# The first block's keys move from SyncE's queue to GpSimd's, in an attention-and-MLP kernel whose order is a searched list

## The chip, the cores and the metric

The program runs on one core of one Trainium2 chip. The metric is the device time in microseconds (us) of one execution. Three executions of the kernel before took 229.1, 229.35 and 229.35 us.

The engines are called PE (TensorE), DVE (VectorE), ACT (ScalarE), POOL (GpSimd) and SP (SyncE). Each runs its own instructions strictly in the order in which they were written, and a wait holds up everything that is queued behind it on that engine. DMAs are issued from two queues here: POOL's, where each issue is itself an instruction that takes 0.5 to 0.9 us of POOL, and SP's.

## The reference

```
scores = (q @ k.T) / sqrt(64)                # 4 batches, 8 heads, 768 positions, 64 wide
keep   = key is one of the first 4, or is among the 128 up to and including the query
a      = softmax(where(keep, scores, -1e9))
x      = (a @ v), heads side by side         # 3072 x 512
h      = x @ w_in                            # 512 x 2048
g      = h * sigmoid(1.702 * h)
out    = g @ w_out                           # 2048 x 512
```

Inputs and output are fp32; the kernel computes its matrix products in fp16.

## The kernel before

**Tiles.** There are 24 blocks of 128 positions, six to a batch. A window of 128 means that a block needs its own keys, those of the block before it in its batch, and the four "sink" keys of the batch. The kernel takes the blocks in the order `ORDER` = 0, 6, 12, 18, 1, 2, 3, ...: the four first blocks of the batches, which have no block before them, come first. This text counts blocks by their **place** in that order, 0 to 23, and writes q3, k3, v3 for the loads of place 3. Two places make a group for the MLP, 12 groups in all. The loads of w_in and w_out come in four quarters each: i0 to i3 and o0 to o3.

**One place, from end to end.** POOL loads q, k and v; such a load turns fp32 into fp16 on its way. Queries and keys are transposed: by PE with a copy by DVE or ACT (places 0 to 7, "tq", L398 and L405, copies at L355 and L359) or by a DMA of SP (L433). PE makes the scores (L481, "own" and, from place 4 on, "prv" for the block before, and L510 for the sinks). DVE merges the two halves (L527), takes maxima (L537, L554, L557) and subtracts them (L578, L602). ACT takes the exponential (L617). The result is transposed by PE (places 0 to 5, L657) or by a DMA of SP ("at", L682); POOL zeroes what the window leaves out (L620, L624). PE multiplies with v (L715, L719, and L709 for the sinks, "av"), DVE divides by the sum (L726, L727, "xn"), and a second transpose follows, by PE (L745) or, for two places at once, by a DMA of SP ("xT", L758).

**The MLP of a group.** PE multiplies with w_in (L780, "hT", steps of 16 or 8 matmuls), ACT applies the gate (L810; for places 0 and 1 ACT takes a tanh at L794 and DVE finishes at L801), PE multiplies with w_out (L834, "o", steps of four matmuls), DVE or ACT copies the sum out (L355, L359) and SP sends it to DRAM.

**Buffers.** The scores' PSUM tile "own" exists once: the next place's scores may start only when DVE has subtracted the maxima of the place before. "mm", for hT, o and transposes, exists three times. POOL's DMAs in flight are limited: the trace shows POOL waiting, before a new issue, for an earlier load to land.

**What sets the order.** Nothing is scheduled when the program is built. A list `SEQUENCE` of 834 operations names, for each, its number and its engine (p PE, a ACT, d DVE, t POOL, s SP), and the kernel emits them in just that order. The list was found by a search off the chip that used the costs in the calls of `plan.add` (cost on the engine, `xfer` for a transfer, `post` for the delay until its data may be used). The costs themselves emit no instruction.

**The first block's keys.** In the kernel before, `hw=["k0"]` sends k0 another way than all other loads: SP loads it as fp32 into a tile of its own, `raw_k` (L263), and DVE rounds it to fp16 (L271, in `round16`). q0 and the other loads of places 0 to 3 are issued by POOL at L277 (128 rows of 512 values), later ones of q and k at L284, of v at L255, w_in at L293, w_out at L302.

Of the kernel before, what the change touches and what calls it, by code (L numbers as in the profile page):

```python
# [27 lines left out]
PE, ACT, DVE, POOL, SP = "PE", "ACT", "DVE", "POOL", "SP"  # L28
# [8 lines left out]
    gbatch={},  # L37
    tanh=(0, 1),
    last=(256, 128, 128),
    hw=["k0"],  # L40
    big=(0, 1, 2, 3),
    avb={0: ("mi", "mm"), 1: ("mi", "mm"), 2: ("mi", "mm")},
    hb={},
# [4 lines left out]
    slack={'v': 1, 's': 1, 'x': 1, 'e': 0.0, 'p': 0.0},  # L48
    steady=8,
    after=8.0,  # L50
    loads="q0 q1 k1 q2 k2 q3 k3 v0 v1 i0 i1 v2 v3 i2 i3 o0 o1 q4 k4 v4 o2 q5 k5 v5 o3".split(),
)
RING = dict(qkn=4, qkt=4, qk0=2, e32=4, a16=4, at=4, atp=4, xn=2, xt=4, gt=3, osb=4, mm=3, own=1, pv=1, mi=1, th=2)

SEQUENCE = """
0s 10d 4d 37s 12t 7d 14t 11a 16t 13t 106p 38d 15t 9d 2d 103p 6d 23t 3d 101p 104a 20t 126p 102a 18t 107p 127d 17t
124p 19t 108d 149p 109d 125a 22t 147p 150a 110d 129p 25t 148a 130p 111d 112a 105t 131d 113a 114p 132d 170p 115a 26t
116p 133d 171a 118p 152p 21t 117a 119d 153p 135a 134d 29t 120p 8d 137p 136a 121d 172p 33t 138a 154d 122p 173a 30t  # L60
139p 156d 123a 175p 155d 174t 140a 141p 481p 142d 158a 24t 157d 143p 176p 482a 144d 160p 34t 159a 483d 145p 161a 27t
177d 162p 484p 163a 146d 28t 179d 166p 487p 485a 167d 181a 486d 493p 488a 178d 489d 490p 40t 494a 180d 39t 478p 491a
495d 182a 32t 492d 183p 164p 479a 165d 499p 36t 184a 480d 185p 42t 500a 187p 195p 186d 193p 501d 48t 189p 196a 496p
190d 194a 168p 188d 497a 217p 215p 197p 169a 498d 218a 198p 191p 43t 199d 514p 192a 508p 216d 515a 200d 518p 46t
201d 509p 519a 31t 202d 239p 502p 240a 52t 203d 219p 128t 237p 221d 503p 238a 204a 520p 67t 222d 220p 510p 5d 223d
93s 504p 225d 224d 1s 242p 49t 94s 511p 151d 226a 45t 505p 512d 241p 521a 51t 506d 516p 243d 54t 524p 517a 244d 205p
525a 528p 206d 253p 245d 529a 255p 207t 522p 254d 247d 256a 246d 530p 35t 523a 227p 97t 208p 248a 228d 258p 257p
209d 270s 531p 259d 210t 230p 532p 260d 231a 229t 211p 261d 526p 249s 232t 212d 533p 527a 263d 262d 44t 233p 60t
536p 234d 264a 55t 213p 534d 537p 214d 41t 271p 538p 50t 273d 265s 235p 250t 539p 236a 274d 272p 548p 540a 296s 275d
550p 276d 57t 549a 552p 58t 277d 283p 53t 553a 544p 285d 551a 266t 554p 545a 286d 284p 251p 555a 287d 542p 61t 252d  # L70
546p 47t 288d 267p 56t 547a 556p 543a 268d 564p 289d 557a 269s 278a 558p 541s 297p 559p 299d 290a 565p 279s 300d
298p 566p 535s 301d 560p 96s 302d 291s 567p 303d 309p 304a 280t 95s 561p 311d 568a 305s 310p 578p 562d 570p 312d
579a 322s 292t 576p 98d 281p 571a 572p 66t 282d 584p 306t 313d 573a 507s 577a 513s 293p 585a 580p 294d 64t 574p 314d
581a 295s 84t 592p 575a 315d 316a 63t 307p 593p 59t 308d 586p 73t 317s 582p 72t 594p 99t 583a 587p 70t 323p 604p
325d 348s 595p 605a 326d 588p 596a 318t 324p 600p 327d 328d 589p 601a 598p 329d 65t 590d 335p 591s 78t 608p 563s
337d 62t 612p 609a 338d 69t 599a 336p 602p 613a 68t 339d 319p 603a 341d 340d 82t 606p 76t 620p 320d 607a 85t 342a
614p 100d 321s 79t 610p 361p 75t 330a 621p 343s 363d 91t 615p 611a 364d 331s 362p 616p 365d 622p 367d 366d 617p 623p
618a 632p 374s 624d 638p 636p 344t 639a 349p 637a 630p 351d 350p 626p 631a 352d 332t 345p 627a 634p 633a 346d 628p
353d 81t 640p 354d 629a 635a 333p 368a 648p 334d 642p 355d 347s 375p 356a 643p 569s 377d 641a 376p 357s 649p 378d
644p 369s 379d 650p 380d 645p 625s 656p 619s 646d 597s 381d 387p 358t 657a 400s 662p 389d 668p 663a 370t 651p 669a  # L80
359p 652a 388p 654p 360d 77t 658p 390d 74t 660p 659a 391d 80t 655a 371p 393d 392d 661a 71t 664p 372d 676p 665a 382a
373s 401p 670p 403d 647s 402p 671p 404d 394a 383s 666p 405d 677p 667a 406d 395s 672p 407d 413p 408a 673p 415d 384t
684p 674d 678p 416d 685a 409s 414p 679p 90t 417d 426s 692p 87t 680d 385p 418d 693a 396t 696p 419d 386d 686p 682p 88t
687a 397p 410t 683a 690p 697a 398d 688p 691a 399s 698p 689a 420a 694p 411p 699p 412d 695a 421s 700p 427p 675s 710p
429d 452s 712p 711a 430d 428p 701p 713a 422t 431d 720p 432d 724p 721a 702d 439p 725a 86t 433d 718p 441d 92t 716p
719a 442d 83t 440p 714p 717a 89t 423p 715a 732p 434a 424d 704p 443d 425s 445d 733p 444d 435s 722p 446a 705p 723a
681s 465p 447s 706p 467d 734p 703s 468d 466p 750p 436t 469d 735p 751a 470d 707p 736a 448t 742p 708a 746p 743a 437p
747a 738p 438d 748p 471d 739a 449p 749a 740p 472a 450d 744p 451s 453p 726p 745a 473s 455d 727p 456d 737s 454p 728p
741a 653s 457d 760p 459d 458d 752p 474t 729p 753a 460a 761p 730d 772p 762p 773a 461s 766p 763p 767a 780p 764a 770p
475p 462t 771a 768p 781a 476d 776p 769a 778p 777a 788p 779a 463p 774p 464d 782p 775a 477s 789p 765s 783p 731s 784p  # L90
790p 785p 796p 786d 791p 797a 754p 792a 808p 793s 709s 794p 787s 809a 802p 795a 755p 803a 806p 756p 807a 798p 800p
799a 757p 801a 804p 758d 822p 759s 805a 810p 816p 811p 823p 812p 824p 813p 817p 814a 825p 818p 826a 815s 828p 819p
827s 829p 820d 830p 831p 821s 832a 833a
"""


# [69 lines left out]
def kernel(  # L166
# [28 lines left out]
    plan = Plan(RING)  # L195
# [26 lines left out]
    def by(e):  # L222
        return nc.sync if e == SP else nc.scalar
# [19 lines left out]
    )  # L243

    def sw(key, cost, fn, xfer, **kw):
        return plan.add(POOL, key, cost, fn, xfer=xfer, post=0.9, **kw)

    ld, qkn = {}, {}

    def load_block(which, b, key, after=0.0):  # L250
        bb, r = divmod(b, 6)
        pair, i = divmod(PLACE[b], 2)
        src = {"q": q, "k": k, "v": v}[which][bb, :, r * P : (r + 1) * P, :].rearrange("h s d -> s h d")
        if which == "v":
            return sw(key, 0.88, lambda b=b, x=2: nc.gpsimd.dma_start(v65[:, b, :, 0:D], src), 0.88 if pair < 4 else 0.95, deps=[z_1], after=after)  # L255
        w = "qk".index(which)
        buf = qkn[pair]
        if which + str(PLACE[b]) in CFG["hw"]:
            raw = const.tile([P, H * D], FP32, name=f"raw_{which}{b}")
            n = CFG["hw"].index(which + str(PLACE[b]))  # L260
            src = {"q": q, "k": k}[which][bb, :, r * P : (r + 1) * P, :].rearrange("h (t e) d -> t h (e d)", e=8)
            got = plan.add(
                {SP: 0.45, ACT: 0.6}, -120 + n, 0, lambda e, src=src, raw=raw, x=9: by(e).dma_start(raw, src), xfer=0.75, post=0.6  # L263
            )

            def round16(e, b=b, w=w, i=i):
                dst, src = buf()[:, i, w].rearrange("p h d -> p (h d)"), raw
                if e == ACT:
                    nc.scalar.copy(out=dst, in_=src)
                else:  # L270
                    (nc.vector if e == DVE else nc.gpsimd).tensor_copy(out=dst, in_=src)  # L271

            return plan.add({DVE: 0.42, ACT: 0.6, POOL: 0.8}, -110 + n, 0, round16, deps=[got], take=[buf])
        if PLACE[b] in CFG["big"]:
            return sw(
                key, 0.64,
                lambda b=b, w=w, i=i: nc.gpsimd.dma_start(  # L277
                    buf()[:, i, w].rearrange("p h d -> p (h d)"),
                    {"q": q, "k": k}["qk"[w]][bb, :, r * P : (r + 1) * P, :].rearrange("h (t e) d -> t h (e d)", e=8),
                ),  # L280
                0.7, take=[buf], after=after,
            )
        return sw(
            key, 0.88, lambda b=b, w=w, i=i: nc.gpsimd.dma_start(buf()[:, i, w], src), 0.88 if pair < 4 else 0.95,  # L284
            take=[buf], after=after,
        )
# [4 lines left out]
    def load_w_in(f, key):  # L291
        def go(f=f, x=0):
            nc.gpsimd.dma_start(  # L293
                w_in16[:, :, bass.ts(f, 512)],
                moe_w_in.rearrange("(c p) f -> p c f", p=P)[:, :, bass.ts(f, 512)],
            )

        return sw(key, 0.8, go, 2.5)

    def load_w_out(f, key):  # L300
        def go(f=f, x=1):
            nc.gpsimd.dma_start(  # L302
                w_out16[:, bass.ts(f, 4)],
                moe_w_out[bass.ts(f, 512), :].rearrange("(c p) f -> p c f", p=P),
            )

        return sw(key, 0.8, go, 2.5)

    for n, what in enumerate(CFG["loads"]):
        w, x = what[0], int(what[1:])  # L310
# [2 lines left out]
        key = -100 + n  # L313
# [581 lines left out]
```

## Time and profile before

| | us |
|---|---|
| three timed executions, median | 229.35 (229.1 to 229.35) |
| the profiled execution, its own time | 228.31 |
| its span in the profile | 226.6 |
| PE busy | 214.5 (95%) |
| DVE busy, ACT busy, POOL busy | 136.2, 136.6, 113.5 |
| granted TensorE clock | 1.0 |
| DMA queue 0 (POOL's loads) | 79.6% of 16 engines |
| DMA queue 1 (SP's) | 44.7% of 16 engines |

The times of single instructions below come from the one profiled execution, whose own time is 1.04 us under the median; differences are worked out inside the profile and then added to the median. "Busy" time of PE counts matmuls that overlap, so that the mean duration of a group (257 ns for one matmul of hT) is more than it costs when matmuls follow each other: eight hT matmuls in a row take 0.87 us and four of o 0.86 us in the chain of waits.

### The profile page before, as it was taken

To read this page: it belongs to the slowest core of one execution; us is meant where nothing else is said; L and a number is where in the kernel's file an instruction comes from. 1 tells how busy PE (TensorE), PEld (TensorE's weight loads), DVE (VectorE), ACT (ScalarE), POOL (GpSimd) and SP (SyncE) were. 2 spreads that over 40 slices of the span, in tenths; PEclk is the share of its full clock that TensorE was granted. 3 is DMA by queue.
4 is the path that set the end of the run, shared out by engine and by line. 5 is a ranking of instruction groups with operands and counts; after the bars stand their busy time and mean duration, and the time that the engine had idled before them with its cause. 6 is when DMAs were issued, how large, how long until landed. Compare 5 with 4: busy or idle time off the path is not lost.

```text
span 226.6 us, 5625 instructions
## 1 busy us (share of the span) xinstructions
PE 214.5 (95%) x2378; PEld 151.7 (67%) x2378; DVE 136.2 (60%) x243; ACT 136.6 (60%) x190; POOL 113.5 (50%) x135
## 2 busy tenths in 40 slices
PE   1889899999999999999899999999999999999994
PEld 0658876776784785675675685686765956856763
DVE  0899898998896852796286677843957371111010
ACT  2588696796746766367349249848585669613511
POOL 8955654698980689397071670780816112300000
PEclk9999999999999999999999999999999999999999
DMA  6999999999999999999998998999998072042112
GB/s 128 174 205 196 178 191 191 156 142 137 134 164 157 203 210 156 120 219 134 148 174 133 260 138 144 127 147 130 150 116 198 4 191 38 17 138 77 66 46 93
DMA packets 123512, 32.47 MB, mean 143 GB/s; under 512 B 114880, under 2 KB 120416, under 8 KB 123488
## 3 DMA queue, kind: packets, MB, share of 16 engines
q0 software_dynamic: 71792, 13.51, 79.6%
q1 hardware_dynamic: 51552, 18.55, 44.7%
q8 instruction: 18, 0.29, 0.6%
q10 hardware_dynamic: 144, 0.07, 0.1%
q14 instruction: 6, 0.05, 0.1%
HBM read 27.46 MB, written 6.29 MB: 149 GB/s over the span
## 4 chain that ended last, share of the span: by engine, by line
PE 77%; DMA 10%; POOL 5%; DVE 2%; ACT 1%; SPq 1%; issue 1%; POOLq 0%; DVEq 0%
PE o L834 33%; PE hT L780 31%; DMA w_in<-in_moe_w_in_dram 6%; DMA at<-a 4%; PE own L481 3%; PE av L715 2%; PE av L719 2%; PE av L709 2%; PE prv L481 2%; POOL qkn L277 2%; SPq L682 1%; POOL v L255 1%; POOL w_in L293 1%; PE tq L405 1%; PE snk L510 1%
## 5 line engine op out<-in xcount | busy, mean ns | idle before, releaser
L780 PE MATMUL hT<-xT,w_in 128*128 128x256 f16 (+1 forms) x896 | 94.1, 257 | 1.4 <-DMA xT<-xn 0.6
L834 PE MATMUL o<-w_out,gT 128*128 128x512 f16 (+2 forms) x416 | 91.8, 363 | 0.0
L810 ACT ACTIVATE gT<-hT 128x512 f16<-128x512 f32 x88 | 50.9, 597 | 58.7 <-PE hT L780 58.4
L780 PEld LDWEIGHTS <-w_in 128*128 128x128 f16 x896 | 75.3, 98 | 14.5 <-DMA xT<-xn 1.1
L834 PEld LDWEIGHTS <-gT 128*128 128x128 f16 x416 | 37.2, 98 | 32.2
L620 POOL TENSOR_SCALAR_AFFINE_SELECT atp<-at 128x1024 f16<-128x1024 f16 (+1 forms) x22 | 22.2, 1009 | 65.7 <-DMA at<-a 64.7
L527 DVE COPY_PREDICATED own<-consts,prv 128x1024 f32<-128x1024 uint16 x20 | 24.6, 1229 | 24.3 <-PE prv L481 24.2
L537 DVE TENSOR_REDUCE mx<-own 128x8 f32<-128x1024 f32 (+1 forms) x28 | 29.7, 1068 | 0.9 <-PE own L481 0.4
L578 DVE TENSOR_TENSOR e<-own,mx 128x1024 f32<-128x1024 f32 (+1 forms) x28 | 29.8, 1066 | 0.9
L617 ACT ACTIVATE a<-e 128x1056 f16<-128x1056 f32 (+1 forms) x28 | 26.2, 952 | 4.9 <-issue 2.6
L624 POOL TENSOR_SCALAR_AFFINE_SELECT at<-at 128x1024 f16<-128x1024 f16 (+1 forms) x22 | 22.5, 1024 | 1.5
L355 DVE COPY osb<-o 128x512 f32<-128x512 f32 (+1 forms) x12 | 8.0, 666 | 24.3 <-PE o L834 24.3
L284 POOL DMA_DIRECT2D qkn<-in_k_dram x20 | 17.8, 902 | 7.4 <-DMA w_out<-in_moe_w_out_dram 5.1
L255 POOL DMA_DIRECT2D v<-in_v_dram x24 | 21.4, 902 | 0.0
L726 DVE RECIPROCAL rcp<-av 128x8 f32<-128x8 f32 (+1 forms) x28 | 5.5, 195 | 26.5 <-PE av L719 26.4
L284 POOL DMA_DIRECT2D qkn<-in_q_dram x20 | 17.8, 894 | 2.3 <-DMA qkn<-in_k_dram 0.7
L810 ACT ACT_TABLE_LOAD x14 | 18.0, 1283 | 0.2
L727 DVE TENSOR_TENSOR xn<-av,rcp 128x512 f16<-128x512 f32 (+1 forms) x28 | 17.2, 615 | 1.0
L715 PE MATMUL av<-v,at 128*128 128x65 f16 x192 | 17.0, 194 | 0.6 <-POOL at L624 0.5
L617 ACT ACT_TABLE_LOAD x13 | 16.7, 1283 | 0.2
L715 PEld LDWEIGHTS <-at 128*128 128x128 f16 x192 | 14.2, 98 | 2.5 <-POOL at L624 1.2
L481 PEld LDWEIGHTS <-qkT 64*128 64x128 f16 x352 | 10.2, 96 | 7.8 <-issue 5.1
(56 smaller groups left out, 165.9 us busy)
## 6 DMA issues: line engine op xcount, KB each, us to landing
out_dram<-osb SPq DMA_DIRECT2D x23, 256.0 KB, 2.5
qkn<-in_q_dram POOLq DMA_DIRECT2D x24, 128.0 KB, 5.3
v<-in_v_dram POOLq DMA_DIRECT2D x24, 128.0 KB, 5.6
qkn<-in_k_dram POOLq DMA_DIRECT2D x23, 128.0 KB, 8.6
w_in<-in_moe_w_in_dram POOLq DMA_DIRECT2D x4, 512.0 KB, 10.2
w_out<-in_moe_w_out_dram POOLq DMA_DIRECT2D x4, 512.0 KB, 11.6
at<-a SPq DMA_TRANSPOSE x18, 3.3
raw_k<-in_k_dram SPq DMA_DIRECT2D x1, 256.0 KB, 4.6
```

What stands on the lines that cost most here:

```text
L255: return sw(key, 0.88, lambda b=b, x=2: nc.gpsimd.dma_start(v65[:, b, :, 0:D], src), 0.88 if pair < 4 else 0.95, deps=[z_1], after=after)
L284: key, 0.88, lambda b=b, w=w, i=i: nc.gpsimd.dma_start(buf()[:, i, w], src), 0.88 if pair < 4 else 0.95,
L527: nc.vector.copy_predicated(out=own(lo, hi).rearrange("p l j s -> p (l j) s"), mask=later.unsqueeze(1).to_broadcast((P, 4 * (hi - lo), P)) ...
L537: lambda lo=lo, hi=hi, own=half, small=small: nc.vector.tensor_reduce(out=small[:, lo:hi], in_=own(lo, hi), axis=AX.X, op=ALU.max),
L578: nc.vector.tensor_tensor(out=e32()[:, 512 * lo : 512 * hi].rearrange("p (l j s) -> p l j s", j=4, s=P), in0=own(lo, hi), in1=small[:, lo: ...
L617: nc.scalar.activation(out=a16()[:, lo:hi], in_=e32()[:, lo:hi], func=AF.Exp, scale=scale)
L620: nc.gpsimd.affine_select(out=atp()[:, lo : lo + n], in_=at()[:, lo : lo + n], pattern=[[0, n], [-1, P]], compare_op=ALU.is_gt, fill=0.0, ...
L624: nc.gpsimd.affine_select(out=at()[:, lo : lo + n], in_=at()[:, lo : lo + n], pattern=[[0, n], [1, P]], compare_op=ALU.is_ge, fill=0.0, ba ...
L715: nc.tensor.matmul(acc[:, j], at()[:, c], v65[:, b, h], start=(r == 0), stop=(r == 0))
L780: nc.tensor.matmul(ht()[:, n], w_in16[:, c, bass.ts(f, P)], xt[g]()[:, tok, c], start=(c == 0), stop=(c == 3))
L810: lambda fs=fs, cols=cols, gt=gt, ht=ht: nc.scalar.activation(out=gt()[:, fs[0] : fs[-1] + 1, cols], in_=ht(), func=AF.Gelu_apprx_sigmoid),
L834: nc.tensor.matmul(po(), gt()[:, F, bass.ts(t, P)], w_out16[:, F, cols], start=(F == 0), stop=(F == NF - 1))
```

## The change

k0 is loaded by POOL like the other keys, at L277, as POOL's first DMA, and lands as fp16. SP's load L263 and DVE's cast L271 are gone (their code stays, unused). Some costs that only the search reads were changed, and the list was searched again: it has 833 operations on the same engines, with another order on each of them.

```diff
-    hw=["k0"],
+    hw=[],
...
-    loads="q0 q1 k1 q2 k2 q3 k3 v0 v1 i0 i1 ...".split(),
+    loads="q0 k0 q1 k1 q2 k2 q3 k3 v0 v1 i0 i1 ...".split(),
...
-        return plan.add(POOL, key, cost, fn, xfer=xfer, post=0.9, **kw)
+        return plan.add(POOL, key, cost, fn, xfer=xfer, **{"post": 1.1, **kw})
...
-                {SP: 0.45, ACT: 0.6}, ... by(e).dma_start(raw, src), xfer=0.75, post=0.6
+                {SP: 0.45, ACT: 0.6}, ... by(e).dma_start(raw, src), xfer=0.9, post=0.6
...
-                key, 0.64,                     # q and k of places 0 to 3
+                key, 0.56,
...
-        return sw(key, 0.8, go, 2.5)           # w_in, w_out
+        return sw(key, 0.8, go, 2.5, post=2.0)
```

The two lists, decoded for the queues that the prediction speaks of. "sink3" is the copy of the sink keys of place 3 (L448), "sel" POOL's zeroing (L620, L624), "tr12" SP's transpose of the queries and keys of places 12 and 13 (L433), "at" L682, "xT" L758.

```
POOL, from the start
  before: q0 k1 k2 q1 q2 v2 v1 k3 q3 v0 i1 i2 sink0 i3 i0 q4 q5 k4 sink3 v3 k5 o0 o1 k6 q6 o2 o3
  after:  k0 q0 k2 q1 q2 k1 k3 q3 v1 v0 i1 i2 i3 v2 sink2 i0 k4 v3 q4 sink1 q5 k5 o0 k6 q6 o1 o2 o3
SP, from the start
  before: consts raw_k ...          after: own-mask consts ...
DVE, from the start
  before: 3 memsets, round k0, 4 memsets, copy k1, maxima and subtractions of place 0 ...
  after:  6 memsets, copy q0, copy k2, maxima and subtractions of place 0 ...
PE, from the start
  before: mask0, tq k0, tq q0, tq k1, own0, tq q1, tq k2, tq q2, mask1, own1 ...
  after:  mask0, tq k0, tq q0, tq k2, own0, tq q1, tq k1, tq k3, mask1, own1 ...
SP, places 8 to 10
  before: at8, at9, at10, tr12 (an output and loads of sink values between)
  after:  at8, at9, tr12, at10, one output ahead of at8
POOL and SP, places 11 to 14
  before: sel11, then 11 loads; SP xT10/11, at13, at12, tr16; POOL sel13, sel12, q20; SP xT12/13
  after:  sel11, then 5 loads; SP at12, xT10/11, at13, tr16; POOL sel12, sel13, then 8 loads; SP xT12/13
POOL and SP, places 16 to 18
  before: SP at16, at17, at18, tr20; POOL sel16, 2 loads, sel17, sel18
  after:  SP at16, at17, tr20, at18; POOL sel16, sel17, sel18
```

More of the change, by code (lines that the diff above doesn't have):

```diff
@@ L50 @@
     after=8.0,
-    loads="q0 q1 k1 q2 k2 q3 k3 v0 v1 i0 i1 v2 v3 i2 i3 o0 o1 q4 k4 v4 o2 q5 k5 v5 o3".split(),
+    loads="q0 k0 q1 k1 q2 k2 q3 k3 v0 v1 i0 i1 v2 v3 i2 i3 o0 o1 q4 k4 v4 o2 q5 k5 v5 o3".split(),
 )
@@ L57 @@
 SEQUENCE = """
[L58 to L92, printed above, removed]
@@ L93 @@
-827s 829p 820d 830p 831p 821s 832a 833a
+1s 6d 0s 4d 13t 3d 12t 17t 14t 2d 8d 10d 16t 11a 15t 105p 19t 18t 102p 21t 100p 103a 20t 148p 101d 23t 106p 149d 26t
+123p 107d 125p 27t 124a 9d 108d 171p 126a 24t 109d 128p 110d 129p 111a 7d 172a 130d 113p 169p 112a 131d 146p 114a
+133d 147a 115p 117p 132d 116a 151p 150t 118d 134a 119p 152p 120d 22t 170a 154d 135a 121p 31t 136p 122a 174p 156d
+175p 25t 137a 153d 138p 480p 177d 139a 30t 155d 158a 142p 483p 127t 481a 143d 157a 482d 140p 34t 484a 159p 141d 161p
@@ new lines @@
+160a 35t 485d 162a 163p 176d 144p 28t 486p 145a 178d 39t 165p 179d 492p 487a 166d 180a 488d 493a 182p 181a 5d 494d
+489p 38t 92s 183d 29t 184p 490a 477p 185d 33t 491d 188p 192p 478a 164d 194p 37t 186p 498p 193a 479d 104t 195a 187d
+495p 499a 189d 42t 167p 500d 496a 196p 41t 168a 216p 497d 214p 190p 217a 198d 513p 191a 60t 197p 215d 507p 514a 199d
+173t 517p 200d 48t 518a 501p 201d 51t 236p 238p 202d 218p 239a 44t 508p 237a 220d 203a 219p 519p 221d 502p 32t 222d
+509p 223d 503p 224d 240p 225a 45t 510p 520a 47t 504p 511d 36t 242d 241p 523p 505a 53t 527p 243d 524a 50t 204p 528a
@@ new lines @@
+521p 244d 40t 205a 246d 245d 515p 522a 96t 254p 516a 252p 206t 529p 255d 247a 253d 207p 226p 269s 208d 256p 209t
+530p 258d 227a 525p 259d 228t 229p 526a 210p 248s 230d 257p 531p 211d 231t 535p 260d 262d 54t 261d 232p 46t 536p
+233d 263a 52t 532p 43t 234p 533d 270p 537p 249t 272d 235a 264s 212p 271p 538p 213a 273d 547p 62t 539a 274d 549p 540s
+275d 548a 295s 551p 276d 282p 265t 550a 555p 284d 543p 556a 94s 285d 552a 283p 57t 250p 93s 544a 286d 541p 59t 251d
+545p 49t 542a 287d 266p 56t 546a 553p 267d 74t 557p 288d 554a 268s 277a 296p 558p 298d 512s 297p 559p 299d 289a 278s
@@ new lines @@
+563p 98t 300d 560p 301d 290s 564p 561d 321s 565p 302d 303a 308p 279t 577p 310d 569p 304s 578a 97d 566p 291t 311d
+534s 280p 567a 579p 281d 77t 573p 580a 78t 292p 574a 309p 570a 583p 58t 312d 293d 575p 305t 584a 313d 294s 571p 581p
+572a 55t 306p 582a 63t 591p 576a 307d 66t 585p 314d 315a 61t 322p 603p 65t 324d 592p 325d 604a 316s 593p 323p 594p
+506s 326d 328d 607p 327d 595a 586p 347s 608a 599p 334p 600a 601p 317t 336d 568s 611p 602a 337d 335p 605p 612a 69t
+338d 597p 606a 340d 72t 339d 318p 598a 81t 587p 329a 319d 68t 609p 71t 360p 588p 341a 330s 362d 619p 610a 589d 320s
@@ new lines @@
+361p 620p 363d 613p 364d 621p 365d 342s 614p 622p 331t 562s 615p 95s 623d 348p 624s 616p 373s 350d 343t 625p 366d
+351d 349p 635p 626a 617a 631p 352d 85t 636a 637p 632a 75t 344p 70t 627p 345d 83t 633p 354d 628a 64t 332p 634a 67t
+639p 638a 333d 80t 629p 353d 346s 76t 647p 630a 640a 374p 355a 641p 376d 648p 377d 642p 367a 356s 375p 649p 378d
+379d 650p 590s 368s 667p 380d 651a 386p 668a 596s 643p 388d 399s 357t 661p 389d 644p 662a 655p 645a 369t 387p 663p
+656a 390d 358p 664a 659p 73t 359d 653p 84t 391d 370p 79t 654a 392d 657p 660a 371d 665p 99d 658a 372s 381a 400p 669p
@@ new lines @@
+646s 402d 675p 403d 393a 401p 382s 670p 404d 666a 676p 405d 394s 671p 406d 425s 412p 407a 677p 414d 383t 413p 683p
+415d 672p 684a 416d 678p 408s 395t 418d 384p 673a 681p 385d 695p 679d 396p 680s 696a 685p 682a 397d 409t 687p 417d
+686a 398s 691p 89t 689p 692a 688a 86t 410p 690a 697p 90t 419a 411d 715p 82t 693p 87t 716a 698p 420s 426p 674s 699p
+428d 694a 652s 719p 429d 427p 711p 720a 451s 430d 709p 712a 431d 421t 717p 710a 432d 438p 718a 713p 440d 439p 703p
+714a 441d 723p 442d 422p 724a 444d 700p 433a 423d 721p 443d 424s 704p 701d 445a 434s 464p 731p 722a 466d 446s 465p
@@ new lines @@
+705p 467d 732p 468d 706p 470d 435t 469d 733p 707a 747p 708s 749p 91t 734p 447t 750a 748a 436p 735a 739p 437d 88t
+745p 448p 746a 741p 740a 449d 743p 450s 737p 744a 742a 618s 452p 738a 725p 454d 751p 455d 759p 752a 471a 453p 726p
+456d 457d 775p 760p 458d 459a 472s 727p 776a 761p 460s 728p 762p 729d 771p 473t 763a 767p 769p 768a 461t 474p 770a
+777p 772a 475d 765p 778a 773p 766a 462p 774a 787p 463d 781p 476s 779p 730s 788p 780a 702s 782p 764s 789p 783p 790p
+797p 791a 784p 792s 798a 736s 803p 785d 805p 786s 804a 795p 806a 807p 796a 793p 808a 801p 794a 799p 802a 821p 800a
@@ L94 @@
+753p 822p 809p 754p 823p 755p 824p 810p 825a 826s 815p 811p 816p 812p 756p 813d 817p 814s 757a 827p 818p 758s 828p
+819d 829p 830p 820s 831a 832a
 """
@@ L262, in load_block @@
             got = plan.add(
-                {SP: 0.45, ACT: 0.6}, -120 + n, 0, lambda e, src=src, raw=raw, x=9: by(e).dma_start(raw, src), xfer=0.75, post=0.6
+                {SP: 0.45, ACT: 0.6}, -120 + n, 0, lambda e, src=src, raw=raw, x=9: by(e).dma_start(raw, src), xfer=0.9, post=0.6
             )
@@ L305, in go @@
             )
-        return sw(key, 0.8, go, 2.5)
+        return sw(key, 0.8, go, 2.5, post=2.0)
     for n, what in enumerate(CFG["loads"]):
```

## The prediction

> **What bounds the kernel now.** The page first: the span, the engines' shares and the slices.
>
> ```profile
> span 226.6 us, 5625 instructions
> ...
> PE 214.5 (95%) x2378; PEld 151.7 (67%) x2378; DVE 136.2 (60%) x243; ACT 136.6 (60%) x190; POOL 113.5 (50%) x135
> ...
> PE   1889899999999999999899999999999999999994
> ...
> DMA  6999999999999999999998998999998072042112
> ```
>
> PE is the bound: away from the first slices and the last it hardly rests, at a granted clock of 1.0. DMA is full in nearly every slice up to about 170 us. The change takes no matmul away, so the time can move only by PE's idle stretches. The waits of PE show which there are:
>
> ```profile
> PE own L473 <- DMA consts<-cconst: 2.9, 1, 2.9
> PE tq L398 <- DVE qkn L271: 2.4, 1, 2.4
> PE hT L780 <- DMA xT<-xn: 0.6, 1, 0.6
> PE hT L780 <- DMA w_in<-in_moe_w_in_dram: 0.6, 1, 0.6
> ...
> PE av L715 <- POOL at L624: 0.5, 1, 0.5
> ```
>
> The second is what the change is about. Fourth: PE at 23.45 waits for the last quarter of w_in. Third and fifth lie in the middle. I added up the gaps between PE's matmul starts beyond what such a matmul takes in a dense run: some 10.4 us from the first matmul on, of them about 8.3 before 28 us, 0.32 at 61.09, 0.80 at 109.67, 0.69 at 115.6, 0.24 at 119.2, and nothing of note after that. Now the head, from the timeline:
>
> ```profile
> 1.22 0.75 SPq L263 DMA_DIRECT2D raw_k<-in_k_dram  x1
> 1.32 0.68 POOL L277 DMA_DIRECT2D qkn<-in_q_dram  x1 [0.80 <-POOLq L876]
> ...
> 5.81 0.43 DVE L271 CAST qkn<-raw_k 128x512 f16<-128x512 f32 x1 [3.94 <-DMA raw_k<-in_k_dram]
> ...
> 6.29 1.07 PE L398 MATMUL tq<-consts,qkn 128*64 128x64 f16 x32 [2.40 <-DVE qkn L271]
> ...
> 8.18 0.61 PE L481 MATMUL own<-qkT 64*128 64x128 f16 x8
> ```
>
> **The change, part by part: the start.** raw_k goes out at 1.22, lands 4.6 us later at 5.8, is cast, and its transpose starts at 6.29. POOL's first load (now q0) goes out at 1.32 and lands 4.2 us later (the landing time of that row), at 5.5. k0 takes that slot: transpose at about 5.55, 0.7 us earlier. q0 is now second; the second load, out at 1.99, landed 4.2 to 4.3 us later, at 6.2, ahead of the 6.3 to 6.8 at which q0 was transposed so far. Its copy is DVE's first (0.69 us), so that own0 starts at 6.2 + 0.5 + 0.2 + 0.7 + 0.15 = 7.75 instead of 8.18: 0.4 us. Without the 256 KB of raw_k beside it k0 may land up to half a us sooner; if POOL's start is slower, nothing is gained. So own0 gains 0 to 0.9, 0.4 taken. consts moves behind the own-mask on SP (one issue, 0.4 us): the mask matmuls then end near 4.3, before k0.
>
> The Trainium skill (DMA: Bandwidth & Descriptors, Specifications) puts the first byte of a POOL load at about 1 us and of an SP load at about 0.6, which speaks against the move; by it k0 would land 0.4 us later than raw_k and the gain would be the cast alone. The trace disagrees: 4.2 us for POOL's load, 4.6 for SP's.
>
> **Where that goes.** DVE's busy time in the windows:
>
> ```profile
> 12.00:16.00 4.00, 3.21 (x65) 2.04 (x64) 3.90 (x11) 3.40 (x8) 1.81 (x3) 1.00 1.25 208
> 16.00:20.00 4.00, 3.46 (x52) 2.68 (x52) 3.93 (x9) 3.51 (x7) 2.84 (x5) 1.00 1.24 206
> 20.00:24.00 4.00, 3.44 (x64) 3.25 (x62) 3.94 (x9) 2.86 (x5) 1.05 (x2) 1.00 1.92 175
> ```
>
> (third pair: DVE.) From 12 to 24 us DVE is full. Its 0.43 us of cast lay before that stretch and is worth nothing by itself; an earlier own0 moves the stretch forward. But w_in paces PE too. Ahead of i0 in POOL's queue there were 13 loads and raw_k beside them, now 14, of the same kinds: i0, out at 10.41 and landed 13.0 us later, lands at 23.4 again. Two moves in that queue need cover. i0 is now issued behind sink2, which waits for a copy that ACT reaches after both exponentials of place 0, so at about 13 us instead of 10.41; the loads ahead of it keep DMA busy to about 20, which hides it (without that cover, 2.6 us). v2 now follows i1 to i3. The loads up to it are those that were up to i3 before, which landed at 20.6 (9.68 + 10.9), so v2 lands near 20.6 instead of 9.1; PE reaches place 2's values at about 19 and stands 1.5 us, but has by then done the w_in step that it did in that time before. At 23.45 PE is ahead by one values step and one transpose (0.36 us). Then q4, behind k4 and v3, lands at 26.1 (v3, four loads behind i0, landed at 27.06: 0.91 each, times three) and holds PE 0.5. Place 5's scores stand 0.7 us of PE work earlier in the list, but need DVE's subtraction of place 4 to free "own": it ended at 34.66, and ends 0.4 earlier at best. At place 6, PE's clock time less the work in front of it is 11.5 us instead of 11.6. I take 0.2 us of gain for the head, from 0.8 gained to 0.5 lost.
>
> **The middle.** The list is new there as well. For both lists I added PE's work between two points (0.88 per hT step, 0.86 per o step, 0.55 for two scores, 0.72 for av) and compared it with the slack that the trace shows. From the last matmul that gates the exponential on ACT to av:
> - place 8: 10.9 us before, now 9.9; POOL's zeroing ended 1.1 us before av. Place 9: 13.3, now 12.4; slack 0.8. Place 10 keeps 16.7 with slack 0.4, but its "at" now stands behind tr12, an issue of 3.2 us at 77.98. Place 11: 15.1, now 13.4; slack 1.9. Together 0 to 2.2, 0.7 taken.
> - places 12 and 13, and hT of group 5: the waits of 0.69, 0.24 and 0.80 arose here:
>
> ```profile
> 101.22 1.24 SPq L758 DMA_TRANSPOSE xT<-xn  x1
> 103.60 7.06 SPq L682 DMA_TRANSPOSE at<-a  x2
> ```
>
> xT took 8.4 us to land and two "at" 7.06 to issue (elsewhere 1.3 each), while POOL issued 11 loads at 96.8 to 106.4. Now 5 loads stand there, and av11 to hT has 10.7 us instead of 9.3. Of the 1.73 us I give back 1.2 (0 to 1.73).
> - The 8 loads taken out stand ahead of xT12/13. From av12 to group 6's hT there are 7.6 us; one us for DVE and 5.7 (xT at 67.83, beside loads) to 8.4 make 6.7 to 9.4. Loss 0 to 1.8, 0.8 taken.
> - places 16 to 18: av17 to group 8's hT has 5.1 us instead of 6.5. Before, av17 ended at 151.0, xT went out at 152.0 and landed 5.0 later, at 157.0; hT began at 157.4. So 1.4 less leaves 0.9 of waiting; a 3.0 us landing (xT at 200.14) would leave none, a later av17 (12.5 us of cover instead of 14.2, slack 0.8) up to 2. at18 now stands behind tr20 (3.6 us at 145.74): 0 to 0.6. I take 1.1 together.
>
> Places 19 to 23 keep slacks of 0.8 us or more (2.3 to 5.6 before), and the tail ends in the same instructions.
>
> **Sum.** −0.2 − 1.2 + 0.7 + 0.8 + 1.1 = +1.2 us; a wait early in a chain relieves those behind it, so I take off 0.5 for that overlap: +0.7. The profiled span goes from 226.6 to 227.3, its own time from 228.31 to 229.0, the median from 229.35 to 230.05. About 0.2% (0.46 us) is what a measurement of this kernel can tell from no change.
>
> **Rivals.**
> 1. *Faster.* The burst of 11 loads was the whole cause in the middle. Then all 1.73 come back, the shorter margins hold because landings are near 3 us rather than 5, and the head keeps 0.2: 229.35 − 1.9 plus some 0.6 of small waits, 228.0. For it: these are the only large waits after 28 us. Against: av17 and xT16/17 were within 0.8 and 0.4 us of waiting. It decides where xT16/17 lands within 4.1 us of its issue. Chance 0.30.
> 2. *No difference.* w_in and w_out pace the head and what the middle gives back equals what it adds: 229.35. For it: DMA is full to 170 us and carries the same bytes. Chance 0.17.
> 3. *Much slower, in the head.* v2 behind three weights, or i0 behind sink2, costs PE outright: each us that v2 lands after 20.6 is a us. At 22.1: 229.35 + 0.7 + 1.5 = 231.5. Against: DMA works off its queue in order of issue so far. Chance 0.08.
> 4. *POOL is held at its first issue.* DVE's memsets now run beside k0's issue, the one of 0.93 us (L231) among them; held for that long, k0 lands at 6.4, own0 starts at 8.6, and the head loses 0.4: 230.6, inside my forecast. Against: that memset ran at 6.62 beside a POOL issue that took 0.94 us, where its equals took 0.95 and 0.97. The Trainium skill (SBUF — State Buffer) warns of such a hold for POOL's descriptors while DVE runs in certain fast modes; that row shows none.
>
> That k0 would not go the new way is excluded: the built program issues it as POOL's first DMA.
>
> **Numbers.** Forecast, slower by its own mechanism: 0.45, with rival 3 0.53 for slower by over 0.2%; within 0.2% 0.17; faster 0.30. The range: from 228.2 (most of the rival's gain) to 231.9 (the middle's upper bounds halved, or rival 3).
>
> **What would show it.** First tq between 5.1 and 5.8 and own0 near 7.7; w_in's last hT again near 23.4; PE waiting for xT before group 8's hT and for POOL before one of av8 to av11; the wait at 109.67 gone. If hT of groups 6 and 8 start without a wait, rival 1 holds and I am wrong; if first tq is later than 6.3, the start is.

## The result, and the profile after

| | before | after |
|---|---|---|
| median of 20 executions each, us | 228.74 (227.82 to 229.87) | 229.73 (228.82 to 231.7) |
| ratio | | 1.0054, 95% interval 1.0032 to 1.0075 |
| the profiled execution, own time / span, us | 228.31 / 226.6 | 231.31 / 229.6 |

The changed kernel is slower by 0.5%, about 1.0 us. Its profiled execution was 1.6 us above its own median and that of before 0.4 below its own, so the two profiles lie 3.0 us apart where the medians lie 1.0 apart: what the profile after shows is read below for where time goes, and the runs say how much.

The page after:

```profile
span 229.6 us, 5625 instructions
...
PE 215.8 (94%) x2378; PEld 152.6 (66%) x2378; DVE 133.2 (58%) x235; ACT 135.4 (59%) x193; POOL 114.6 (50%) x138
...
PE   3687999999999899999999799999999999999994
...
DMA  6999999999999999999999999969927735063003
```

The same 2378 matmuls. PE's first digits are 3687 where they were 1889: it starts sooner and is then less busy until about 23 us. The waits of PE (total, times, longest, in us):

```profile
PE own L473 <- DMA consts<-cconst: 3.4, 1, 3.4
PE tq L398 <- DMA qkn<-in_k_dram: 2.1, 2, 1.5
PE av L715 <- DMA v<-in_v_dram: 1.2, 1, 1.2
PE hT L780 <- DMA xT<-xn: 1.2, 1, 1.2
PE av L715 <- POOL at L624: 1.1, 2, 0.9
```

The wait for DVE's cast is gone. In its place PE waits for keys that POOL loads, then for v2; in the middle one wait is for xT and two are for POOL. The head, from the timeline (start, length, engine):

```profile
1.32 0.68 POOL L277 DMA_DIRECT2D qkn<-in_k_dram  x1 [0.80 <-POOLq L876]
1.99 0.54 POOL L277 DMA_DIRECT2D qkn<-in_q_dram  x1
...
4.46 1.26 PE L398 MATMUL tq<-consts,qkn 128*64 128x64 f16 x32
...
7.25 0.64 PE L398 MATMUL tq<-consts,qkn 128*64 128x64 f16 x16 [1.54 <-DMA qkn<-in_k_dram]
...
7.83 0.61 PE L481 MATMUL own<-qkT 64*128 64x128 f16 x8
...
21.95 0.28 PE L715 MATMUL av<-v,at 128*128 128x65 f16 x4 [1.18 <-DMA v<-in_v_dram]
```

k0 and q0 land 3.1 and 3.0 us after their issues, both are transposed in one run from 4.46, and then PE stands 1.5 us: its next instruction is the transpose of k2, and k2, out at 2.51, lands only 4.7 us later. own0 is queued behind it. DVE in the windows shown before:

```profile
12.00:16.00 4.00, 3.49 (x66) 2.31 (x60) 3.53 (x9) 2.97 (x6) 3.05 (x6) 1.00 1.25 207
16.00:20.00 4.00, 3.75 (x62) 3.10 (x62) 3.93 (x9) 3.76 (x9) 1.75 (x2) 1.00 1.42 197
20.00:24.00 4.00, 2.76 (x49) 2.56 (x50) 3.79 (x9) 2.76 (x7) 1.64 (x2) 1.00 1.68 186
```

(third pair.) DVE is still nearly full, but PE's share of 20 to 24 us fell from 3.44 to 2.76. In the middle, the places where the largest waits stood before, and the two where they stand now:

```profile
104.48 1.75 SPq L682 DMA_TRANSPOSE at<-a  x1
106.33 2.62 SPq L758 DMA_TRANSPOSE xT<-xn  x1
...
120.79 2.08 SPq L758 DMA_TRANSPOSE xT<-xn  x1
```

```profile
80.57 0.20 PE L715 MATMUL av<-v,at 128*128 128x65 f16 x1 [0.95 <-POOL at L624]
...
128.65 1.03 PE L780 MATMUL hT<-xT,w_in 128*128 128x256 f16 x8 [1.18 <-DMA xT<-xn]
```

xT10/11 lands 4.6 us after its issue instead of 8.4, and the waits at 109.67, 115.6 and 119.2 are gone. xT12/13, out at 120.79 behind eight loads, now takes 7.8 us and holds group 6's hT; place 8's mask holds av8.

To compare kernels I use three numbers from each trace, counted like all times here from the program's first instruction. **own0**: when PE starts the first scores. **Four loads**: when POOL's queue has moved its first 512 KB. **Through i0**: when POOL's queue has moved all loads up to and with i0 (3328 KB as written; 128 more where k0 is among them, 128 fewer where q0 isn't), summed over the DMA packets. The recorded expectations below count this last mark from an earlier zero, 0.3 to 0.7 us ahead of the first instruction and not the same in each trace, so their figures for it lie that much higher. And for PE, **lost time**: from 0 to 30 us, the stretch less what its matmuls take in a dense run; from 40 to 140 us, where PE hardly rests, the sum of the gaps over 0.2 us beyond a dense run.

| | own0 | four loads | through i0 | PE lost, 0 to 30 us | 40 to 140 us |
|---|---|---|---|---|---|
| before | 8.18 | 6.77 | 21.74 | 11.6 | 2.1 |
| after | 7.83 | 7.00 | 22.81 | 12.7 | 3.5 |

### The profile page after: what moved, and what is told of

Same layout as the page of the kernel before. It is cut to its first block, busy times and chain, and to the rows that moved or that the text cites. A ratio compares the mean times of both kernels' runs of the same rounds, so it can differ in the third digit from the quotient of the medians.

```text
span 229.6 us, 5625 instructions
## 1 busy us (share of the span) xinstructions
PE 215.8 (94%) x2378; PEld 152.6 (66%) x2378; DVE 133.2 (58%) x235; ACT 135.4 (59%) x193; POOL 114.6 (50%) x138
## 4 chain that ended last, share of the span: by engine, by line
PE 74%; DMA 13%; POOL 5%; DVE 3%; ACT 2%; issue 1%; POOLq 0%; SPq 0%
PE hT L780 33%; PE o L834 29%; DMA xT<-xn 6%; DMA v<-in_v_dram 5%; PE av L715 2%; PE own L481 2%; DMA at<-a 2%; PE av L719 2%; POOL qkn L277 2%; PE av L709 2%; PE prv L481 2%; ACT a L617 1%; POOL w_in L293 1%; PE tq L405 1%; POOL v L255 1%
## 5 line engine op out<-in xcount | busy, mean ns | idle before, releaser
L780 PE MATMUL hT<-xT,w_in 128*128 128x256 f16 (+1 forms) x896 | 93.0, 257 | 1.8 <-DMA xT<-xn 1.2
L834 PE MATMUL o<-w_out,gT 128*128 128x512 f16 (+2 forms) x416 | 90.6, 363 | 0.0
L620 POOL TENSOR_SCALAR_AFFINE_SELECT atp<-at 128x1024 f16<-128x1024 f16 (+1 forms) x22 | 22.2, 1010 | 67.8 <-DMA at<-a 57.5
L617 ACT ACTIVATE a<-e 128x1056 f16<-128x1056 f32 (+1 forms) x28 | 26.1, 950 | 4.9 <-issue 2.4
L624 POOL TENSOR_SCALAR_AFFINE_SELECT at<-at 128x1024 f16<-128x1024 f16 (+1 forms) x22 | 22.5, 1024 | 1.5
L355 DVE COPY osb<-o 128x512 f32<-128x512 f32 (+1 forms) x10 | 6.6, 661 | 28.0 <-PE o L834 24.6
L359 ACT COPY osb<-o 128x512 f32<-128x512 f32 (+1 forms) x14 | 7.6, 540 | 19.1 <-PE o L834 17.4
```

Of the source, the lines that this page charges most:

```text
L617: nc.scalar.activation(out=a16()[:, lo:hi], in_=e32()[:, lo:hi], func=AF.Exp, scale=scale)
L620: nc.gpsimd.affine_select(out=atp()[:, lo : lo + n], in_=at()[:, lo : lo + n], pattern=[[0, n], [-1, P]], compare_op=ALU.is_gt, fill=0.0, ...
L624: nc.gpsimd.affine_select(out=at()[:, lo : lo + n], in_=at()[:, lo : lo + n], pattern=[[0, n], [1, P]], compare_op=ALU.is_ge, fill=0.0, ba ...
L780: nc.tensor.matmul(ht()[:, n], w_in16[:, c, bass.ts(f, P)], xt[g]()[:, tok, c], start=(c == 0), stop=(c == 3))
L834: nc.tensor.matmul(po(), gt()[:, F, bass.ts(t, P)], w_out16[:, F, cols], start=(F == 0), stop=(F == NF - 1))
```

## Experiments

The kernels were timed in five rounds each beside the kernel before, but for the one with a quarter in third place; the ratios are to the kernel before in the same session.

**Path and order apart.** The change does two things that can be done one at a time: k0 by POOL, and the new list.

Path alone, in the order of before:

```diff
-    hw=["k0"],
+    hw=[],
-POOL: q0 k1 k2 q1 q2 v2 ...      SP: consts raw_k ...     DVE: 3 memsets, round k0, ...
+POOL: k0 q0 k1 k2 q1 q2 v2 ...   SP: consts ...           DVE: 3 memsets, ...
```

> The order of before, with one thing changed: k0 is POOL's first load instead of SP's fp32 load and DVE's cast. Theory H (the new order, not the new path, costs the time): first tq near 4.5 instead of 6.3, own0 earlier by 0.4 to 1.5, the last quarter of w_in and the middle as before; total 0 to 0.8 us under before. Rival P (the path costs: one more issue of 0.54 us in POOL's queue and one more load in it, everything behind comes later): own0 no earlier or the quarters of w_in later by over 0.5, total 0.5 to 1.2 us over before, and the order alone without the path would be no slower than before.

Measured: 230.06, ratio 1.0065 (1.0031 to 1.0098). In its profile i0 lands at 23.74 instead of 23.41, and PE, which runs the same matmuls in the same order as before, is 0.36 us behind at 30 us. Most of the rest is lost in the middle, near 116 us, at the masks of places 12 and 13 (0.5 us before):

```profile
PE av L716 <- POOL at L625: 1.3, 2, 1.1
```

Order alone, with k0 by SP and DVE as before:

```diff
-    hw=[],
+    hw=["k0"],
-POOL: k0 q0 k2 ...   SP: own-mask consts ...          DVE: 6 memsets, copy q0 ...
+POOL: q0 k2 ...      SP: consts raw_k own-mask ...    DVE: 6 memsets, round k0, copy q0 ...
```

> The order of after, with k0 loaded and cast the old way (SP, then DVE behind its six memsets; the own-mask of SP behind it). Theory H: as slow as after or slower, 1.0 to 2.5 us over before, with the same waits (v2 near 22, place 8's av, xT before group 6's hT). Rival P: back to before within 0.4 us.

Measured: 228.84, ratio 1.0010 (0.9981 to 1.0038). Theory H falls: the new list alone costs nothing that can be measured (0.4% at most), and the path alone costs as much as the whole change. Its profile still has the waits in the middle:

```profile
PE av L716 <- POOL at L625: 1.0, 2, 0.8
PE hT L781 <- DMA xT<-xn: 0.9, 2, 0.6
...
PE av L716 <- DMA v<-in_v_dram: 0.6, 1, 0.6
```

so those are in the new order with either path, and what the list gives elsewhere must pay for them.

**The changed kernel's head.** Two changes to its list, each at a wait that its profile shows.

```diff
-PE: tq k0, tq q0, tq k2, own0      DVE: copy q0, copy k2, maxima of place 0
+PE: tq k0, tq q0, own0, tq k2      DVE: copy q0, maxima of place 0, copy k2
```

> After, with place 0's scores ahead of tq k2 on PE, and the copy of k2 behind place 0's two maxima on DVE. Theory H says that the start was handed back there: own0 near 6.6 instead of 7.8. If DVE's stretch paces the head, the total falls by 0.5 to 1.2 us; if v2 and w_in pace it, as the wait of 1.2 us for v2 says, place 2's values still start near 22 and the total is that of after within 0.3 us. I expect the second.

Measured: 229.90, ratio 1.0047 (1.0019 to 1.0075).

```diff
-POOL: ... v1 v0 i1 i2 i3 v2 sink2 i0
+POOL: ... v1 v0 v2 i1 i2 i3 sink2 i0
```

> After, with the load of v2 ahead of the quarters of w_in (behind v0) instead of behind three of them. Theory H: the wait of 1.2 us for v2 near 22 is gone, i1 to i3 land 0.9 later, i0 as before; total 0.5 to 1.2 us under after. Rival W (w_in paces the head in any order): PE waits for i3 or i0 instead, total that of after within 0.3 us.

Measured: 230.13, ratio 1.0059 (1.0032 to 1.0086). Neither moves the time. Scores ahead of k2's transpose gain nothing, so the 1.5 us before 7.25 is not what the kernel pays for. v2's wait is gone in the second one's trace, with nothing gained: PE waits 0.5 us for a quarter of w_in instead, as rival W said, and POOL's queue is through i0 no sooner (22.99 against 22.81).

**Where the path costs.** The windows of the DMA engines (last two columns: busy share of an engine, and GB/s moved). Before, with SP's 256 KB of raw_k beside POOL's first loads:

```profile
3.00:4.50 1.50, 0.90 (x2) 0.00 (x0) 0.00 (x0) 0.00 (x0) 1.50 (x4) 1.00 0.91 204
4.50:7.00 2.50, 0.71 (x26) 0.71 (x28) 1.03 (x5) 0.03 (x1) 2.50 (x5) 1.00 1.22 212
```

After:

```profile
3.00:4.50 1.50, 1.08 (x4) 0.18 (x6) 0.09 (x3) 0.20 (x1) 1.50 (x4) 1.00 1.08 157
4.50:7.00 2.50, 1.21 (x32) 0.96 (x32) 0.69 (x1) 0.58 (x1) 2.50 (x5) 1.00 1.02 116
```

The path alone, then the order alone:

```profile
4.50:7.00 2.50, 1.21 (x34) 0.94 (x35) 0.00 (x0) 1.17 (x2) 2.50 (x5) 1.00 1.03 128
```

```profile
4.50:7.00 2.50, 0.53 (x20) 0.53 (x22) 0.43 (x1) 0.00 (x0) 2.46 (x5) 1.00 1.21 208
```

POOL is issuing all the time in all four (fifth pair). Yet with k0 on POOL's queue the engines move 116 to 128 GB/s between 4.5 and 7.0 us, against 208 to 212; single packets of POOL's queue last up to 1.0 us there, where the usual one lasts about 0.1. The difference isn't only SP's own bytes: of the 212 and 208, POOL's queue alone moved 185 and 173. From 3.0 to 4.5 us it is the other way round, 157 and 159 for POOL's queue when it is alone, 74 and 63 beside SP's load. I called it the slow stretch, and asked what makes it. The first guess was that POOL's queue, alone on the engines, overtakes POOL. A load on SP's queue that nothing uses should then cure it:

```diff
 SP: own-mask, consts, ...
+SP: consts, k0 once more as fp32 into a tile that is not read, own-mask, ...
```

> The changed kernel as it is, and beside it SP loads the first block's keys once more, in fp32, into a tile that nothing reads, right behind its load of the constants (the own-mask behind it, as in the kernel before). Nothing of the computation is left out. In the profiles with k0 on POOL's queue that queue moved 50 to 70 packets per half microsecond between 4.5 and 7.0, single packets lasting up to 1 us; with the fp32 load of k0 on SP's queue it moved about 100 from 5.0 on and no packet lasted over 0.33 us. Theory C (POOL's queue, alone on the 16 engines, works off its first loads faster than POOL hands over the next, and each time that it has caught up costs it): with SP's 256 KB beside it, it never catches up; 90 to 100 packets per half microsecond from 5.0 on, no long packets, k0 and q0 later by 0.5 to 1.0 and the later q and k loads sooner; time 228.6 to 229.3 against 228.5 for before. Rival D (the slow stretch belongs to k0 being POOL's load, for whatever reason, and extra bytes only add to it): the slow stretch stays, everything in the head 0.7 later, time 230.0 to 230.8.

Measured: 229.90, ratio 1.0063 (1.0036 to 1.0090). The windows:

```profile
3.00:4.50 1.50, 0.98 (x2) 0.07 (x2) 0.09 (x3) 0.20 (x1) 1.50 (x4) 1.00 0.90 179
4.50:7.00 2.50, 1.26 (x32) 1.02 (x32) 0.00 (x0) 0.58 (x1) 1.97 (x4) 1.00 1.19 212
```

The slow stretch is gone, as theory C said, and the time is not better, as it did not say: four loads are done at 7.03 and all through i0 at 22.60, where it was 7.00 and 22.81 without the extra 256 KB. With half of the rows:

```diff
-    extra = const.tile([P, H * D], FP32)          # 128 rows, 256 KB
+    extra = const.tile([P // 2, H * D], FP32)     # 64 rows, 128 KB
```

> The changed kernel with an extra fp32 load on SP's queue that nothing reads, as in the run with an extra load, but of half the rows (64 partitions, 128 KB). Nothing of the computation is left out. With no extra load POOL's queue has done all loads through i0 at 23.24, with 256 KB extra at 23.26, where the slow stretch of 4.5 to 7.0 was gone and the extra bytes had taken its place. That catching up with POOL makes the stretch fell with the quarter in third place (24.28). If any bulk transfer on SP's queue beside POOL's first two loads keeps the stretch away: no packet over 0.5 us after 5.0, loads through i0 done at 22.7 to 23.0 (half the extra's 0.64 less than 23.26), own0 near 8.0, time 229.0 to 229.6. If it takes the whole 256 KB, or the effect goes with the size: a stretch that is still there, through i0 at 23.2 or later, 229.6 to 230.3.

Measured: 230.40, ratio 1.0051 (1.0020 to 1.0083); half a stretch:

```profile
4.50:7.00 2.50, 1.49 (x40) 1.22 (x42) 0.27 (x1) 0.58 (x1) 2.50 (x5) 1.00 1.18 174
```

and through i0 at 22.71. None, 128 or 256 KB beside POOL's first loads: the mark is 22.81, 22.71 and 22.60, no later for the added bytes. The bytes on SP's queue are carried in time that POOL's queue doesn't use. Theory C itself was put to the test with a long load early:

```diff
-POOL: k0 q0 k2 q1 q2 k1 k3 q3 v1 v0 i1 ...
+POOL: k0 q0 i1 k2 q1 q2 k1 k3 q3 v1 v0 ...
```

> The changed kernel with w_in's second quarter (512 KB, 2.6 us of the queue for 0.75 us of POOL) moved up to be POOL's third load, ahead of k and q of the second block. Its use is one mark, the moment at which POOL's queue has done all loads through i0; the start is later by design. Theory C (the queue loses time between 4.5 and 7.0 because it has caught up with POOL): behind a quarter it can't catch up, no packet over 0.5 us after 4.5, all loads through i0 done at 22.1 to 22.5. Rival D (the slow stretch belongs to k0 on POOL's queue): still a slow stretch, done at 23.0 to 23.5. Time 229.5 to 232 by either.

Measured, in one execution: 234.22, through i0 at 23.93, later than either theory had it, and

```profile
4.50:7.00 2.50, 1.25 (x32) 1.01 (x32) 0.69 (x1) 0.58 (x1) 2.50 (x5) 1.00 0.93 122
```

The stretch is there, and goes on to about 10 us. A queue with 2.6 us of work in hand hasn't caught up with POOL, so theory C falls.

If one load on SP's queue rides for nothing, two might:

```diff
-    hw=[],
+    hw=["k0", "q0"],          # SP: consts, k0, q0, own-mask; DVE rounds k0, ACT rounds q0
```

> The changed order, with both k0 and q0 loaded by SP in fp32 and rounded, k0 on DVE and q0 on ACT. If what costs the changed kernel is that POOL's queue has to bring k0 (and so all loads behind it come later), then one load fewer on it brings k1 to k3, q1 to q3 and v0 sooner by another 0.6: own0 near 8.0, losses of the head 10.5 to 11.5 (11.5 with only k0 on SP), time 228.0 to 228.9. Rival: two fp32 loads of 256 KB share SP's queue and the 16 engines, k0 or q0 lands after 6.0, own0 is at 8.8 or later, time 229.2 to 230.0.

Measured: 229.70, ratio 1.0044 (1.0015 to 1.0073): the rival. All through i0 is done at 21.81, hardly sooner than with k0 alone on SP (21.91), so the second load did not ride for nothing, and the start is late:

```profile
6.69 0.64 PE L399 MATMUL tq<-consts,qkn 128*64 128x64 f16 x16 [2.68 <-DVE qkn L272]
8.02 1.07 PE L399 MATMUL tq<-consts,qkn 128*64 128x64 f16 x32 [0.69 <-ACT qkn L270]
9.45 0.61 PE L482 MATMUL own<-qkT 64*128 64x128 f16 x8 [0.36 <-DVE qkT L356]
```

**The waits in the middle.** Four or five loads moved out of the bursts, in the changed kernel and in the one with the order alone (there v2 was put behind v0 as well):

```diff
 POOL: q13 from ahead of sel7 to behind sel9; v21 from the loads ahead of xT12/13 to behind sel14;
       q21 and q20 from there to behind sel15
```

> The changed kernel with four loads moved out of the way of at8 and of the xT of places 12 and 13: q of place 13 behind the two masks of place 9, the v of place 21 behind a mask of place 14, q of places 20 and 21 behind a mask of place 15. Prices the two middle terms of the sum (0.7 at places 8 to 11, 0.8 at group 6's hT; the profile after showed 1.4 and 1.3). If they were paid in full: PE waits under 0.5 for POOL at av8 and for xT at group 6's hT, time 227.6 to 228.6. If the head's loss alone sets the time, or the waits move elsewhere: 229.3 to 230.0.

Measured: 231.46, ratio 1.0124 (1.0088 to 1.0161).

> The changed order with k0 on SP and DVE as before (the kernel that ran at 228.84), and five loads moved: v2 right behind v0, q of place 13 behind the two masks of block 9, v and q of places 20 and 21 (three loads) behind the masks of places 14 and 15. In that kernel's profile PE waited 0.6 for v2, 1.0 for the mask of place 8 (its DMA landed 5 us after issue behind five loads) and 0.9 for an xT (landing 7.8 behind eight loads). If these waits were what set the time, they fall and nothing else comes: 226.5 to 227.8. If what is late next is close behind (as in the changed kernel with v2 early, which did not move): 228.4 to 229.0.

Measured: 230.63, ratio 1.0071 (1.0042 to 1.0101). Both are slower than the kernels that they were made from by 0.6 to 0.7%. Group 6's wait for xT did go in both. But q13 had been issued at 60 us, six microseconds ahead of the burst that stands before at8, so at8 gained nothing, while behind sel9 it pushed sel10: PE's loss at av10 rose from 0.34 to 1.2 us, and a wait for an xT of 0.7 and 0.2 us came after it. I took it that I had moved one load too many. The second attempt left q13 alone:

```diff
 POOL: q17 from ahead of sel8 to beside k17; q19 and k19 from ahead of sel10 to behind q16;
       v21 behind sel14; q21, q20 and k20 behind sel15
```

> The changed order with k0 on SP and DVE as before (the kernel that ran at 228.84), and seven loads moved that lie in the bursts ahead of at8 and of the xT of places 12 and 13 or ahead of the mask of place 10 and are not needed yet: q17 beside k17, q19 and k19 behind the loads that follow the mask of place 11, v21 behind a mask of place 14, q20, k20 and q21 behind a mask of place 15. That kernel's profile showed PE waiting 1.0 at av8, 0.34 at av10 and 0.75 at group 6's hT. The last moves showed that group 6's wait goes when v21, q20 and q21 leave the burst, and that q13 (issued at 60 us) was not what held at8, while behind place 9's masks it cost av10 0.9. If the loads right ahead of at8 are what makes it land 5 us after issue: all three waits gone, 226.8 to 227.8. If at8's landing is set by something else (the transposes of places 8 and 9 issued back to back): only group 6's and av10's go, 227.6 to 228.4.

Measured: 229.13, ratio 1.0016 (0.9989 to 1.0042): no faster than the kernel that it was made from (1.0010), and slower than either forecast.

> The changed kernel with the same seven moves: against the run beside it, it differs in the path of k0 alone, the third such pair. Profiles of the others showed the bytes of POOL's queue through i0 done 1.0 us later with k0 on it (23.0 to 23.5 against 22.0 to 22.3), whatever the order. If that is what the path costs: 0.8 to 1.6 us over the run beside it, 228.0 to 229.2, i0 landed near 23.3. If the path's price depended on the middle's waits: equal to the run beside it within 0.4.

Measured: 229.67, ratio 1.0071 (1.0034 to 1.0107). PE's waits for POOL and xT in the second of them:

```profile
PE av L716 <- POOL at L625: 1.1, 1, 1.1
```

av8, av10 and group 6 wait no more (between 40 and 140 us PE lost 0.4 us, where the changed kernel lost 3.5), but the loads now behind sel14 and sel15 are followed by a new wait of 1.1 us at 147.0, for the masks of place 16. The time is that of the changed kernel. A wait taken out here came back further on.

No kernel of these beats the one before. All that bear on the path, in one table (numbers as defined above):

| k0 | order | own0 | four loads | through i0 | ratio |
|---|---|---|---|---|---|
| SP | before | 8.18 | 6.77 | 21.74 | 1 |
| POOL | before | 7.52 | 6.71 | 22.53 | 1.0065 |
| SP | new | 8.33 | 6.95 | 21.91 | 1.0010 |
| POOL | new (the change) | 7.83 | 7.00 | 22.81 | 1.0054 |
| SP | new, 7 loads moved | 8.18 | 6.91 | 21.84 | 1.0016 |
| POOL | new, 7 loads moved | 7.83 | 6.54 | 22.65 | 1.0071 |
| POOL, and 128 KB on SP | new | 7.48 | 6.90 | 22.71 | 1.0051 |
| POOL, and 256 KB on SP | new | 7.82 | 7.03 | 22.60 | 1.0063 |
| SP, q0 too | new | 9.45 | 7.71 | 21.81 | 1.0044 |

In three orders the path costs 0.65, 0.44 and 0.55%, each give or take 0.3 to 0.5. Each time the first scores start sooner, by 0.35 to 0.66 us, and the kernel is slower: what goes with the time is the moment when POOL's queue is through i0, 0.8 to 0.9 us later. Only q0 on SP is slow with that mark early; its scores start over a microsecond late, and PE is still 1.0 us behind the order alone at 100 us.

The fourth column tells why the mark is late. POOL's queue has moved its first four loads by 6.5 to 7.0 us, by either path. Without SP's load its first one is done 0.6 to 0.8 us sooner (at 3.9), and the slow stretch takes that back. With k0 on SP these four loads are q0 and three more; with k0 on POOL they are k0, q0 and two more. The load on SP's queue was carried for nothing, and put on POOL's it makes one load more for all that follows: at the 194 GB/s that the queue moves from 10 to 23 us, 128 KB take 0.7 us, by estimate.

How the later queue becomes a later end is shown only in part. In each of the three pairs PE runs the same matmuls in the same order, so that the moments of one matmul can be compared. With k0 on POOL's queue PE is behind by 0.36, 1.27 and 0.67 us at 30 us, by 0.36, 1.11 and 0.00 at 100 us, and by 1.32 and 1.70 us at the end, or 0.15 ahead in the third pair. The head pays in all three; what the middle adds or takes back differs between these single executions, and the runs do not say why.

## Why the prediction was right, and where it was not

The time (230.05 against 229.73), the sign and the range held; I gave +0.7 us and +1.0 was measured, since before came out at 228.74 over more executions. The cause did not hold, so that the sum came near is luck: it put the loss into the new list's middle and a gain into the head, and the runs put nothing measurable into the list, and the loss on k0's path, which I had taken for a small gain.

- **The start: right in its result.** own0 was to start at 7.75 and started at 7.83. The way there was another. k0 and q0 landed 3.1 and 3.0 us after issue, not 4.2, so that the first tq came at 4.46, ahead of the 5.1 to 5.8 that I gave; own0 then waited behind the transpose of k2, which landed late. (The aside on first bytes is wrong by its own figures: a landing 0.4 us later takes back the 0.43 us of the cast, so nothing would be gained. The sum doesn't use it.)
- **"i0 lands at 23.4 again": the step that failed.** I counted 13 loads and raw_k before against 14 loads after, and took raw_k for one of the same kind. i0 landed at 24.26, not 23.4; POOL's queue was through it 1.1 us later (22.81 against 21.74), 0.8 with the order kept. raw_k had cost POOL's queue nothing, and k0 cost it one load. The trace of before held the numbers: 204 and then 212 GB/s while two queues ran. It did not show what POOL's queue does alone, and I gave that no bounds.
- **v2 at 20.6:** it landed at 21.8, for the same reason. PE's wait was 1.2 instead of 1.5, since PE came later too; for i0, behind it, PE did not wait at all. q4 landed at 27.0 instead of 26.1, and PE did not wait for it either. Rival 3 had each microsecond beyond 20.6 as a microsecond of time; with v2 moved early the time stayed, so v2 alone was not what decided; the quarters of w_in behind it then came later.
- **Head in sum:** a gain of 0.2 forecast; in the profiles PE lost 12.7 us up to 30 us instead of 11.6, and with the path alone, in the order of before, PE was 0.36 us behind at 30 us.
- **Middle.** Places 12 and 13 and group 5: 1.73 us came back, 1.2 taken. Places 8 to 11: 0.7 taken, 1.4 in the profile (1.11 at av8, 0.34 at av10). Group 6: 0.8 taken, 1.3 in the profile, with xT landing in 7.8 us, inside the 5.7 to 8.4 that I had allowed. Group 8: 1.1 taken, nothing there; its xT landed 3.1 us after issue (at 156.3, with hT at 157.1), under the 4.1 that I gave as the point. These are sizes of one execution, 1.6 us above its kernel's median; the order alone, which has the same list, came out at 1.0010, so their balance with the rest of the list is nearer to nothing than to the +1.4 that I had.
- **Rivals.** "Faster" fell at group 6 and held at group 8. "No difference" is what the list gave by itself. Rival 4, DVE holding POOL at its first issue, fell: k0 landed at 4.4, not 6.4. Nor does DVE make the slow stretch: with the order alone the 0.93 us memset ran beside POOL's first issues as it does after, and the engines moved 208 GB/s; and the path alone was slow while DVE did nothing at all (the 0.00 in its window).

The Trainium skill (DMA: Bandwidth & Descriptors, Rules for kernel authors) says that spreading DMAs over the issuing engines doesn't help bandwidth, since all run on the same 16 engines. By that rule the path would have been neutral, as I forecast for i0. This case's runs disagree for the first microseconds: 128 KB or 256 KB on SP's queue left POOL's queue through i0 at 22.71 and 22.60 against 22.81, and k0 moved from SP's queue to POOL's made that mark 0.8 to 0.9 us later. The measurement decides.

What stays open is what slows POOL's queue when it is alone at the start. It isn't the lack of issued loads (a quarter in third place made it longer), nor DVE. It shrinks with the bytes on SP's queue: 116 GB/s with none, 174 with 128 KB, 212 with 256 KB (of these POOL's queue moved 116, 158 and 169). Open too is how the later queue works through to the end, and why moving loads out of the middle's bursts gained nothing.

## What to carry to other kernels

Where a burst of loads paces the start, ask of each transfer which queue it is on, and not only how many bytes there are: one load on the idle queue can be free (a second one here was not), and moved to the busy one it delays every load behind it. Watch the last load of the burst as well as the first result; here the first scores came up to 0.66 us sooner in kernels that were 0.4 to 0.7% slower. And when a change brings a path and a new order together, run each alone before explaining the sum.

## What was not expected of the hardware

- POOL's DMA queue alone moved 116 to 143 GB/s between 4.5 and 7.0 us of the program, in seven kernels, with single packets of 0.95 us and more; with one 256 KB fp32 load on SP's queue beside it the engines moved 208 to 226 GB/s in five kernels, and no packet of POOL's queue in that window lasted over 0.54 us.
- A load that POOL issued first, at 1.32 us, landed 3.0 to 3.4 us after its issue with nothing beside it and 3.9 to 4.5 us with 256 KB of SP's beside it.
- In the changed kernel a DMA transpose of SP landed 7.8 us after its issue with eight loads issued just ahead of it, 4.6 with five, and 3.0 to 3.3 late in the program; in the kernel before, one amid eleven loads took 8.4.
